# Two head groups taken in turn at the start of an mLSTM, soft-MoE and ReLU² kernel

## The chip, the cores and the metric

One core of a Trainium2 chip runs the whole program. The metric is the device time of one execution in microseconds; less is better.

## The reference

Three layers follow one another on float32 data: an mLSTM over 4 batches of 8 heads (768 steps, head size 40), a soft mixture of experts (8 experts, 4 slots each) and an MLP with a squared ReLU.

```python
for t in range(S):                         # mLSTM, for each batch and head
    m_new = np.maximum(f[t] + m, i[t])
    C = exp(f[t] + m - m_new) * C + exp(i[t] - m_new) * outer(v[t], k[t])
    n = exp(f[t] + m - m_new) * n + exp(i[t] - m_new) * k[t]
    m = m_new
    y[t] = sigmoid(o[t]) * (C @ q[t]) / max(abs(n @ q[t]), 1)
x = y as (3072, 320)
logits = x @ phi                           # soft mixture of experts
slot_in = softmax(logits, over tokens).T @ x
slot_out = relu(slot_in @ w1[e]) @ w2[e]   # e of 8
x = softmax(logits, over slots) @ slot_out
out = relu(x @ w_in)**2 @ w_out            # MLP
```

## The kernel before

The recurrence is computed in chunks of 128 steps, six to a head. The 32 heads form 11 groups of three (the last has two). A **unit** is one chunk of one group; there are 66, and `units` lists them in the order of work: before, group by group, six chunks each. The program writes out the order of every engine's queue by hand; each engine works in that order.

Before any unit, the gates of all heads at once (96 rows: the 32 heads three times) go through phases, for two chunks at a time: `prep(0, 2)`, `prep(2, 4)`, `prep(4, 6)`. The phases have one-letter names: `f` and `m` are scans and `i`, `p`, `a`, `b`, `r`, `l` further steps on VectorE (DVE; some with `G` on GpSimd, POOL), `h`, `A`, `B`, `u`, `v` are passes on ScalarE (ACT), and `q` is a transpose on TensorE (PE) into `qt3`. `D` is a step of the decay (`prep_dec`). The string `START` lists the phases, the steps of the first units and the dummy matmuls (`~n` for n of 128x256, `~~n` for 4n of 40 rows) in order; `|` parts what runs inside the loop, one part at the end of each unit. `M`, `E`, `K`, `T`, `P` with a number are the steps `e_mb`, `e_exp`, `e_sel`, `e_st`, `e_pm` of a unit of group 0.

For unit i the loop emits, in this order: loads for later groups; `e_u(i)`, k times wv (L493); `e_st(i+2)`, keys times queries (L468); `e_mb(i+3)`, the decay products (L437); `e_uc(i)` (L509, L512, VectorE), which takes `u` into the state, and the mask of that state on GpSimd (L528); fillers from later stages; `e_pm(i+2)`, the product of scores and weights (L480, VectorE); `e_exp(i+3)`, three exponentials (L451, ScalarE); `e_av` for two chunks at each second unit (L553); `e_inter(i)` (L538); `e_sel(i+3)`, the causal select (L458, GpSimd); numerators (`e_num`, L571 ScalarE, L572 and L579 VectorE); `e_wv` (L424, GpSimd); the next part of `START`; fillers. `fin` normalises a finished group: `numr` (L613) on GpSimd, then x on VectorE (L622).

PSUM has eight banks here: two each for `mb`, `st` and `o`, one for `m`, one (`ltb`) for the logits, half of which the dummies use. `u` lies in the spare last quarter of the `st` bank of unit i+2.

Group g keeps keys in block-diagonal form (`kbd`), queries, v and k in `par[g % 2]`. A group's keys, queries, v and k are 360, 384, 369 and 360 KB, the two gate files 288 KB each. All DMAs are issued by SyncE (SP) in program order. x arrives per batch, its sigmoid is made on ScalarE (`sigm`, L651), w_in arrives in ten pieces in `stage` and is narrowed (`win_all`, L140 to L152) as the last of the fillers, w1 in sixteen halves (`ring` for experts' first column half, `ring2` for the second) from unit 17 on. Behind the units come the routing of the last batch, the expert layers (w2 reloads `ring` after the first up-projection, L123) and the last MLP (L1387), which is half of the time.

Of the kernel before, what the change touches and what calls it, by code (L numbers as in the profile page):

```python
# [22 lines left out]
GL = 3  # L23
# [9 lines left out]
WO = (4, 5, 9)  # L33
START = "~42 1f 1i 1m 1h 1p 1b 1B 1aG 1r 2f 1u 1A 1v 1q 1l M0 2iG E0 M1 K0 W T0 T1 2m E1 K1 3f 2p 2b 2a ~24 2h 3i 3m 2B Z0 2r 2A 2v 2u P0 3p 3bG D0 3h Z1 ~3 2q ~~5 2l M2 E2 D0 P1 3a 3A 3B K2 D0 D0 3r 3u D0 | 3l 3v 3q | D1 D1 | D1 D1 D1 |"
REBIAS = 2.0**-112
# [7 lines left out]
def kernel(  # L43
# [80 lines left out]

    w1q = [(i, p) for i in range(8) for p in range(2)]

# [64 lines left out]
    ltb = ps.tile([128, 512], F32, name="ps_lt")  # L191
    dum = ltb[:, 256:512]
# [6 lines left out]
    def warm64(n):  # L199
        t = bank("m")  # L200
        for w in (128, 41):
            for _ in range(n):
                for o, r in ((dum, 0), (t, 64)):
                    a = ident[r : r + 40]
                    nc.tensor.matmul(o[:, 0:w], lhsT=a, rhs=a[:, 0:w], start=True, stop=True)

# [14 lines left out]

    def load_kv(g):
        h0, nh = groups[g]
        o = 4 * S
        for dst, src, w in ((vin, v_s, DV), (kin, k_s, D)):
            t = par[g % 2][:, o : o + NC * nh * w]
            o += NC * 3 * w
            dst[g] = t.rearrange("p (c n d) -> p c n d", c=NC, d=w)
            nc.sync.dma_start(out=t, in_=src[S * w * h0 : S * w * (h0 + nh)].rearrange("(p f) -> p f", p=128))

# [49 lines left out]
    nc.sync.dma_start(out=ig.rearrange("p c s -> p (c s)"), in_=i_gate)  # L280
    nc.vector.memset(kbd[0][:, :, 0 : S // 2], 0.0)
    nc.vector.memset(kbd[0][:, :, S // 2 : S], 0.0)
    for cs in (slice(0, S // 2), slice(S // 2, S)):
        load_kb(0, cs)
        load_q(0, cs)
    load_kv(0)
    nc.sync.dma_start(out=phs, in_=phi)
# [29 lines left out]
    nc.vector.tensor_copy(sel96, selF[0:96])  # L317
    nc.vector.tensor_reduce(out=gmask, in_=gj, axis=AX.X, op=ALU.add)
    nc.vector.tensor_reduce(out=gs3, in_=gj.rearrange("p g j -> p j g"), axis=AX.X, op=ALU.add)
    nc.vector.tensor_copy(hsel, gs3.unsqueeze(2).to_broadcast([32, 3, D]))  # L320
    nc.vector.tensor_copy(sel4, selF.unsqueeze(1).to_broadcast([128, 4, 32]))

# [3 lines left out]
    fc = gt(96, [NC, L])  # L326
    dec = gt(32, [NC, 1])
    q3, mm, r1 = ig, fg, dl

    def prep(c0, c1):  # L330
# [11 lines left out]
        def qt():  # L342
            t = bank("o")
            for c in range(c0, c1):
                nc.tensor.transpose(t[:, 96 * (c - c0) : 96 * (c - c0) + 96], q3[:, c, :], ident[0:96, 0:96])
            nc.scalar.copy(qt3[:, cs, :], t[:, 0 : 96 * w].rearrange("p (c s) -> p c s", s=96))
# [69 lines left out]
    ws, pms, pos, cus, cbds = {}, {}, {}, {}, {}  # L416
    units = [(g, c) for g in range(NG) for c in range(NC)]
    NU = len(units)
# [14 lines left out]
    def e_mb(g, c):  # L433
        h0, nh = groups[g]
        mb = bank("mb")
        for j in range(nh):
            nc.tensor.matmul(  # L437
                mb[:, 128 * j : 128 * j + 128],
                lhsT=sel96[:, h0 + j : h0 + j + 1].to_broadcast([96, 128]),
                rhs=M3[:, 128 * c : 128 * c + 128],  # L440
                start=True,
                stop=True,
            )
        mbs[g, c] = mb
# [17 lines left out]
    def e_st(g, c):  # L462
        nh = groups[g][1]
        nd = nh * D
        st = stk.pop(units[max(units.index((g, c)) - 2, 0)], None) or bank("st")
        ts_ = slice(128 * c, 128 * c + 128)
        for j in range(nh):
            nc.tensor.matmul(  # L468
                st[:, 128 * j : 128 * j + 128],
                lhsT=kbd[g % 2][0:nd, j, ts_],  # L470
                rhs=qin[g][0:nd, ts_],
                start=True,
                stop=True,
            )
        sts[g, c] = st
# [12 lines left out]
    def e_u(g, c):  # L488
        nh = groups[g][1]
        nd, nv = nh * D, nh * DV  # L490
        stk[g, c] = bank("st")
        u = stk[g, c][:, 384:512]
        nc.tensor.matmul(  # L493
            u[0:nd, 0:nv],
            lhsT=kin[g][:, c].rearrange("p n d -> p (n d)"),
            rhs=wvs.pop((g, c)).rearrange("p n d -> p (n d)"),
            start=True,
            stop=True,
        )
        us[g, c] = u  # L500

    def e_uc(g, c):
        nh = groups[g][1]
        nd, nv = nh * D, nh * DV
        uv = us.pop((g, c))[0:nd, 0:nv].rearrange("p (n d) -> p n d", d=DV)
        hv = hm[0:nd, 0:nh].unsqueeze(2).to_broadcast([nd, nh, DV])
        cb = wk.tile([120, nh, DV], F32, tag="cbd", name="cbd", bufs=2)
        if c == 0:
            nc.vector.tensor_tensor(out=cb[0:nd], in0=uv, in1=hv, op=ALU.mult)  # L509
        else:  # L510
            cu = wk.tile([120, nh, DV], F32, tag="cu", name="cu", bufs=1)
# [12 lines left out]

# [36 lines left out]
    def e_num(g, c):  # L561
# [282 lines left out]

    def start_exp(c):
        e_mb(0, c)
        e_exp(0, c)
        e_sel(0, c)
# [30 lines left out]
    for i, (g, c) in enumerate(units):  # L879
        if c == NC - 2 and 0 < g + 2 < NG:  # L880
            load_kb(g + 2)
        if i == 0:
            load_kb(1)
        if c == 0 and g + 1 < NG:
            load_q(g + 1)
        if c == 1 and g + 1 < NG:
            load_kv(g + 1)
        if i == 0:
# [23 lines left out]
        if i + 3 < NU:  # L912
            e_mb(*units[i + 3])
# [37 lines left out]
        if i in (0, 2):
            e_wv(0, i + 2, i + 4)
        elif i > 2 and i + 3 < NU and units[i + 3][1] % 3 == 0:
            e_wv(units[i + 3][0], units[i + 3][1], units[i + 3][1] + 3)
        if start:
            run(start.pop(0))
        filler(END, i >= LI)
# [531 lines left out]
```

## Time and profile before

| | |
|---|---|
| three runs | 394.40, 395.84, 396.88 us; median 395.84 |
| profiled execution | 396.85 us, of which the trace's span is 395.1 |
| PE busy | 383.2 us (97%) |
| DVE busy | 264.7 us (67%) |
| ACT busy | 251.9 us (64%) |
| POOL busy | 103.6 us (26%) |
| HBM read | 52.10 MB |

The span runs from the first to the last instruction; 1.75 us of the profiled execution lie outside it. The busy shares are means over stages of quite different kinds, so the rows below are taken by stretch. The chain that ended last runs over PE for 81% of the span.

### The profile page before, as it was taken

The numbers are of one execution on the slowest core, as the hardware profiler recorded it, in microseconds if no ns is written. First come the engines' busy times: TensorE is split into PE (matmuls) and PEld (weight loads), VectorE is DVE, ScalarE is ACT, GpSimd is POOL, SyncE is SP. The second block draws the span as 40 slices with busy tenths as digits, with TensorE's granted clock in tenths as the row PEclk, the third lists the DMA queues.
The fourth block names the chain that finished last, engine by engine and source line by source line (L and its number), as shares of the span: only waits on it lengthen the run. The fifth ranks groups of instructions, "written<-read, shape, count | busy, mean of one in ns | idle before, by whom it ended". The sixth has DMA issues, their size and how long they took to land.

```text
span 395.1 us, 9288 instructions
## 1 busy us (share of the span) xinstructions
PE 383.2 (97%) x3497; PEld 339.0 (86%) x3497; DVE 264.7 (67%) x612; ACT 251.9 (64%) x575; POOL 103.6 (26%) x208
## 2 busy tenths in 40 slices
PE   7998999999999999999998999999999999999996
PEld 5897898889889885534688999999999999999996
DVE  8846787878988786447699856555655655655551
ACT  3676765768677752335598776676666667667662
POOL 6554767747676646200000000000000000000000
PEclk9989999999999999999999999999999999999999
DMA  6577568789889879989100020010001001001001
GB/s 198 171 236 255 190 205 294 268 301 331 275 290 327 238 258 339 327 315 423 73 1 2 0 68 1 2 66 2 1 13 55 2 0 68 0 2 66 2 0 66
DMA packets 18665, 56.62 MB, mean 143 GB/s; under 512 B 2357, under 2 KB 6181, under 8 KB 18237
## 3 DMA queue, kind: packets, MB, share of 16 engines
q1 hardware_dynamic: 18621, 56.04, 41.4%
q8 instruction: 27, 0.44, 0.5%
q14 instruction: 17, 0.14, 0.1%
HBM read 52.10 MB, written 3.93 MB: 142 GB/s over the span
## 4 chain that ended last, share of the span: by engine, by line
PE 81%; DMA 5%; DVE 4%; ACT 3%; POOL 2%; issue 2%; SPq 0%; DVEq 0%; ACTq 0%; POOLq 0%
PE ps_mb L1387 17%; PE ps_st L1387 15%; PE ps_st L468 9%; PE ps_lt L1387 8%; PE ps_o L553 5%; PE ps_o L538 4%; PE ps_o L1311 4%; DMA ring<-in_w_dram 3%; PE ps_st L493 3%; PE ps_mb L437 2%; PE ps_m L668 2%; PE ps_m L1311 2%; PE ps_lt L674 2%; DMA stage<-in_w_in_dram 2%; PE ps_st L1099 1%
## 5 line engine op out<-in xcount | busy, mean ns | idle before, releaser
L1334 DVE CAST hi<-ring 128x512 fp32r<-128x512 f32 x91 | 38.8, 427 | 60.7 <-ACT ring L1333 50.7
L1335 DVE TENSOR_TENSOR lo<-ring,hi 128x512 fp32r<-128x512 f32 x96 | 66.5, 693 | 10.0
L451 ACT ACTIVATE w<-ps_mb,qt 128x128 f32<-128x128 f32 x192 | 56.9, 372 | 23.7 <-PE ps_mb L437 19.4
L1316 ACT ACTIVATE ring<-ps_o 128x512 f32<-128x512 f32 x65 | 38.9, 598 | 36.6 <-PE ps_o L1311 36.5
L1333 ACT ACTIVATE ring<-ring 128x512 f32<-128x512 f32 x91 | 57.5, 632 | 2.9
L468 PE MATMUL ps_st<-par 120*128 120x128 f32 (+1 forms) x384 | 54.6, 278 | 0.0
L1387 PE MATMUL ps_mb<-wohlh,hi 128*128 128x320 f32 x160 | 49.6, 311 | 0.0
L1387 PE MATMUL ps_mb<-wohlh,lo 128*128 128x320 f32 x160 | 49.5, 310 | 0.0
L1387 PE MATMUL ps_mb<-wohll,hi 128*128 128x320 f32 x160 | 49.3, 309 | 0.0
L468 PEld LDWEIGHTS ps_st<-par 120*128 120x128 f32 (+1 forms) x384 | 48.6, 193 | 0.5 <-issue 0.5
L458 POOL TENSOR_SCALAR_AFFINE_SELECT w<-w 128x384 f32<-128x384 f32 (+1 forms) x66 | 36.9, 561 | 37.6 <-ACT w L451 29.3
L1387 PE MATMUL ps_st<-wohlh,hi 128*128 128x320 f32 x144 | 44.8, 311 | 0.0
L1387 PE MATMUL ps_st<-wohlh,lo 128*128 128x320 f32 x144 | 44.7, 310 | 0.0
L1387 PE MATMUL ps_st<-wohll,hi 128*128 128x320 f32 x144 | 44.6, 310 | 0.0
L480 DVE TENSOR_TENSOR p<-ps_st,w 128x384 f32<-128x384 f32 (+1 forms) x66 | 35.5, 538 | 5.3 <-POOL w L458 4.3
L1387 PEld LDWEIGHTS ps_mb<-wohll,hi 128*128 128x128 f32 x160 | 30.1, 188 | 1.3
L1316 ACT ACTIVATE ring<-ps_m 128x512 f32<-128x512 f32 x31 | 18.6, 599 | 18.8 <-PE ps_m L1311 18.8
L1387 PEld LDWEIGHTS ps_mb<-wohlh,hi 128*128 128x128 f32 x160 | 30.0, 188 | 0.0
L1387 PEld LDWEIGHTS ps_mb<-wohlh,lo 128*128 128x128 f32 x160 | 30.0, 188 | 0.0
L553 PE MATMUL ps_o<-par,p 128*64 128x41 f32 x768 | 29.4, 233 | 0.0
L553 PEld LDWEIGHTS ps_o<-par,p 128*64 128x64 f32 x768 | 25.5, 139 | 3.6 <-issue 0.4
L538 PE MATMUL ps_o<-cbd,par 120*128 120x123 f32 (+1 forms) x110 | 25.6, 315 | 3.0 <-POOL cbd L528 2.7
(271 smaller groups left out, 796.3 us busy)
## 6 DMA issues: line engine op xcount, KB each, us to landing
ring<-in_w_dram SPq DMA_DIRECT2D x24, 640.0 KB
stage<-in_w_in_dram SPq DMA_DIRECT2D x10, 512.0 KB
par<-in_w_dram SPq DMA_DIRECT2D x6, 640.0 KB
out_dram<-ring SPq DMA_DIRECT2D x24, 160.0 KB
par<-in_v_s_dram SPq DMA_DIRECT2D x10, 369.0 KB
par<-in_k_s_dram SPq DMA_DIRECT2D x10, 360.0 KB
par<-in_k_t_dram SPq DMA_DIRECT2D x29, 120.0 KB
par<-in_q_t_dram SPq DMA_DIRECT2D x9, 384.0 KB
```

The costliest lines, as they stand in the source:

```text
L451: nc.scalar.activation(w[:, j, :], mb[:, 128 * j : 128 * j + 128], AF.Exp, bias=qt3[:, c, h0 + j : h0 + j + 1])
L458: nc.gpsimd.affine_select(out=w, in_=w, pattern=[[0, nh], [1, 128]], compare_op=ALU.is_ge, fill=0.0, base=0, channel_multiplier=-1)
L468: nc.tensor.matmul(st[:, 128 * j : 128 * j + 128], lhsT=kbd[g % 2][0:nd, j, ts_], rhs=qin[g][0:nd, ts_], start=True, stop=True,)
L480: nc.vector.tensor_tensor(out=p, in0=sts.pop((g, c))[:, 0 : nh * 128].rearrange("p (n t) -> p n t", n=nh), in1=ws.pop((g, c)), op=ALU.mult,)
L538: nc.tensor.matmul(pos[g, c // 2][:, o0 : o0 + nv], lhsT=qin[g][0:nd, 128 * c : 128 * c + 128], rhs=cbds[g, c - 1][0:nd], start=True, stop ...
L553: nc.tensor.matmul(po[t0 : t0 + 64, o0 : o0 + DV], lhsT=p[:, j, t0 : t0 + 64], rhs=vin[g][:, c, j, :], start=True, stop=True,)
L1311: nc.tensor.matmul(t, lhsT=gst[n][:, 128 * k : 128 * k + 128], rhs=cst[tg], start=True, stop=True)
L1316: nc.scalar.activation(r, t, AF.Relu)
L1333: nc.scalar.activation(r, r, AF.Square)
L1334: nc.vector.tensor_copy(hi, r)
L1335: eng.tensor_tensor(out=lo, in0=r, in1=hi.bitcast(F32), op=ALU.subtract)
L1387: nc.tensor.matmul(acc[u][:, 0:DM], lhsT=l_[:, 128 * u : 128 * u + 128], rhs=wohl[r_, f // 8][:, f % 8, :], start=(f == 0 and a == 0), sto ...
```

## The change

The order of units becomes g0c0, g0c1, g1c0, g1c1, g0c2, g0c3, g1c2, g1c3, g0c4, g0c5, g1c4, g1c5, and from group 2 on as before. Group 1's arrays are loaded at the start beside group 0's, group 2's in two pieces at units 6 and 10. Three of the four zero fills of `kbd` are made on ScalarE (a copy scaled by 0). `START` does the phases of chunks 0 to 3, all but `2q`, ahead of the loop and spreads the rest over units 0 to 6; its part in each unit now runs ahead of `e_pm`. It has fewer dummies: 24 + 6 + 6 instead of 42 + 24 + 3 and 20 of 40 rows. `u` moves into the last quarter of the `mb` bank of unit i+3, and `e_mb(i+3)` now stands right behind `e_u(i)`, ahead of `e_st(i+2)`. The gates' transposes use `ltb` instead of an `o` bank. The numerators of groups 0 and 1 lie in `ring`, which w1 fills after `ring2` now; two state buffers for each of the two groups lie in `ring` too. `sigm(0)` is added at unit 4 instead of 0, `win_all` at unit 8 instead of 5.

```diff
-START = "~42 1f 1i 1m 1h 1p 1b 1B 1aG 1r 2f 1u 1A 1v 1q 1l M0 2iG E0 M1 K0 W T0 T1 2m E1 K1 3f 2p 2b 2a ~24 2h 3i 3m 2B Z0 2r 2A 2v 2u P0 3p 3bG D0 3h Z1 ~3 2q ~~5 2l M2 E2 D0 P1 3a 3A 3B K2 D0 D0 3r 3u D0 | 3l 3v 3q | D1 D1 | D1 D1 D1 |"
+START = "~24 1f 1i 1m 1h 1p 1b 1aG 1B 1r 1u 1A 1v D0 S 2f 1l T0 T1 1q M0 2i E0 W0 K0 D0 M1 E1 ~6 2m D0 2p 2b 2aG K1 W2 P0 2h D0 2B 2r 2u P1 M2 E2 2A 2v 2l K2 | 3f 3i ~6 | 2q 3m 3h 3p | 3b 3aG 3B D1 3r | 3u 3A 3l D1 3v D1 D1 | 3q D2 | D2 | D2 D2 X |"
...
-    w1q = [(i, p) for i in range(8) for p in range(2)]
+    w1q = [(i, p) for i in (4, 5, 6, 7, 0, 1, 2, 3) for p in range(2)]
...
-    nc.vector.memset(kbd[0][:, :, S // 2 : S], 0.0)
-    for cs in (slice(0, S // 2), slice(S // 2, S)):
-        load_kb(0, cs)
-        load_q(0, cs)
-    load_kv(0)
+    for g, cs in ((1, halves[0]), (0, halves[1]), (1, halves[1])):
+        z = kbd[g][:, :, cs]
+        nc.scalar.activation(z, ident[0 : 3 * D, 0:1].unsqueeze(2).to_broadcast(list(z.shape)), AF.Copy, scale=0.0)
+    for g in range(2):
+        load_kb(g, halves[0])
+        load_q(g, halves[0])
+        load_kv(g)
+    for g in range(2):
+        load_kb(g, halves[1])
+        load_q(g, halves[1])
...
-            t = bank("o")
+            t = ltb
...
-    units = [(g, c) for g in range(NG) for c in range(NC)]
+    units = [(g, c0 + c) for c0 in range(0, NC, 2) for g in range(2) for c in range(2)]
+    units += [(g, c) for g in range(2, NG) for c in range(NC)]
...
-        mb = bank("mb")
+        mb = mbk.pop((g, c), None) or bank("mb")
...
-        st = stk.pop(units[max(units.index((g, c)) - 2, 0)], None) or bank("st")
+        st = bank("st")
...
-        stk[g, c] = bank("st")
-        u = stk[g, c][:, 384:512]
+        n = units.index((g, c)) + 3
+        t = bank("mb")
+        if n < NU:
+            mbk[units[n]] = t
+        u = t[:, 384:512]
...
+            if g < 2:
+                nums[g] = ring[:, NC * nh * DV * g : NC * nh * DV * (g + 1)].rearrange("p (c n d) -> p c n d", c=NC, n=nh)
+            else:
+                nums[g] = tp.tile([128, NC, nh, DV], F32, tag="num", name="num")
...
+        if i in (6, 10):
+            cs = (0, 4) if i == 6 else (4, NC)
+            load_kb(2, slice(L * cs[0], L * cs[1]))
+            load_q(2, slice(L * cs[0], L * cs[1]))
+            load_kv(2, *cs)
...
         if c < NC - 1:
             e_u(g, c)
+        if i + 3 < NU:
+            e_mb(*units[i + 3])
         if i + 2 < NU:
             e_st(*units[i + 2])
...
-        if i == 5:
+        if i == 8:
             add(win_all(), "win")
...
         if MID:
             filler(MID)
+        if start:
+            run(start.pop(0))
         if i + 2 < NU:
             e_pm(*units[i + 2])
```

## Rows read from the trace of the kernel before

**Rows 1.** Stretches: each engine's busy us (x instructions), granted clock, DMA share, GB/s.
```profile
2.13:17.41 15.28, 14.32 (x135) 12.08 (x133) 14.01 (x37) 6.87 (x22) 9.16 (x24) 1.00 0.64 201
17.41:26.98 9.57, 9.21 (x101) 8.41 (x100) 4.82 (x16) 8.16 (x25) 4.38 (x9) 0.82 0.70 232
26.98:44.17 17.19, 15.19 (x204) 13.98 (x201) 11.26 (x29) 11.21 (x34) 11.13 (x22) 1.00 0.67 220
44.17:142.00 97.83, 97.67 (x1277) 86.74 (x1275) 80.51 (x208) 67.75 (x211) 66.98 (x127) 1.00 0.84 276
142.00:172.00 30.00, 28.59 (x280) 16.81 (x281) 18.53 (x72) 10.87 (x32) 10.55 (x21) 1.00 0.86 301
```

**Rows 2.** VectorE in order of time: start us, us, then what.
```profile
2.44 1.02 DVE L282 MEMSET par<- 120x1152 f32 x1 [0.31 <-DVE par L281]
...
25.57 0.29 DVE L572 TENSOR_TENSOR tmp<-ps_o,qt 128x123 f32<-128x123 f32 x1 [0.42 <-ACT num L571]
...
26.43 0.55 DVE L480 TENSOR_TENSOR p<-ps_st,w 128x384 f32<-128x384 f32 x1
```

**Rows 3.** TensorE in order of time: `u` of units 0, 4, 12.
```profile
17.41 0.47 PE L493 MATMUL ps_st<-wv,par 128*120 128x123 f32 x2
...
27.32 0.38 PE L493 MATMUL ps_st<-wv,par 128*120 128x123 f32 x2
...
44.17 0.37 PE L493 MATMUL ps_st<-wv,par 128*120 128x123 f32 x2
```

**Rows 4.** Who waited for whom, 12 to 45 us: in total, times, longest.
```profile
DVE cu L512 <- PE ps_st L468: 4.4, 4, 1.5
...
PE ps_o L538 <- POOL cbd L528: 1.9, 2, 1.4
```

**Rows 5.** The chain that ended last, in order of time: start us, us, what.
```profile
20.09 1.29 PE ps_st L468 x6
...
27.18 6.40 DMA stage<-in_w_in_dram
...
62.01 0.21 PE ps_st L493 x2
62.22 0.67 PE ps_st L468 x6
62.89 0.17 PE ps_mb L437 x3
63.06 0.83 PE ps_o L553 x24
63.89 0.41 PE ps_o L538 x2
...
65.36 0.27 PE ps_o L538 x2
...
172.48 12.83 DMA ring<-in_w_dram
```

**Rows 6.** Two single microseconds, columns as in rows 1.
```profile
20.00:21.00 1.00, 1.00 (x7) 1.00 (x7) 0.00 (x0) 0.95 (x4) 0.57 (x2) 0.50 0.97 260
168.00:169.00 1.00, 1.00 (x12) 0.26 (x8) 0.94 (x3) 0.00 (x0) 0.00 (x0) 1.00 0.21 87
```

**Rows 7.** ScalarE in order of time, 20 to 36 us.
```profile
21.16 0.74 ACT L651 ACTIVATE x<-x 128x640 f32<-128x640 f32 x1
...
33.60 0.66 ACT L140 ACTIVATE wi<-stage 128x512 f32<-128x512 f32 x1 [3.03 <-DMA stage<-in_w_in_dram]
```

**Rows 8.** All engines, 87 to 90 us.
```profile
88.73 0.88 ACT L451 ACTIVATE w<-ps_mb,qt 128x128 f32<-128x128 f32 x3
...
89.23 0.34 DVE L512 SCALAR_TENSOR_TENSOR cu<-cbd,dec,ps_st 120x123 f32<-120x123 f32 x1 [0.29 <-POOL cbd L528]
```

**Rows 9.** GpSimd in order of time, 0 to 46 us.
```profile
11.54 0.59 POOL L424 TENSOR_TENSOR wv<-par,qt 128x246 f32<-128x246 f32 x1
...
39.41 1.14 POOL L613 TENSOR_TENSOR numr<-num,rc 128x240 f32<-128x240 f32 x2
```

More of the change, by code (lines that the diff above doesn't have):

```diff
@@ L191 @@
     ltb = ps.tile([128, 512], F32, name="ps_lt")
-    dum = ltb[:, 256:512]
+    dum = ltb[:, 0:256]
     zb = ident.bitcast(BF16)
@@ L197, in warm @@
             nc.tensor.matmul(dum if t is None else t[:, 0:256], lhsT=zb[:, 0:128], rhs=zb, start=True, stop=True)
[L199 to L205, printed above, removed]
     kin, vin, xb = {}, {}, {}
@@ L220, in load_q, with load_kv @@
         nc.sync.dma_start(out=par[g % 2][0:n, 3 * S : 4 * S][:, cs], in_=q_t[h0 * D : h0 * D + n, cs])
-    def load_kv(g):
+    def load_kv(g, c0=0, c1=NC):
         h0, nh = groups[g]
@@ L228, in load_kv @@
             dst[g] = t.rearrange("p (c n d) -> p c n d", c=NC, d=w)
-            nc.sync.dma_start(out=t, in_=src[S * w * h0 : S * w * (h0 + nh)].rearrange("(p f) -> p f", p=128))
+            fs = slice(c0 * nh * w, c1 * nh * w)
+            nc.sync.dma_start(
+                out=t[:, fs], in_=src[S * w * h0 : S * w * (h0 + nh)].rearrange("(p f) -> p f", p=128)[:, fs]
+            )
     def load_x(b, cs):
@@ L280 @@
     nc.sync.dma_start(out=ig.rearrange("p c s -> p (c s)"), in_=i_gate)
-    nc.vector.memset(kbd[0][:, :, 0 : S // 2], 0.0)
-    nc.vector.memset(kbd[0][:, :, S // 2 : S], 0.0)
-    for cs in (slice(0, S // 2), slice(S // 2, S)):
-        load_kb(0, cs)
-        load_q(0, cs)
-    load_kv(0)
+    halves = slice(0, S // 2), slice(S // 2, S)
+    nc.vector.memset(kbd[0][:, :, halves[0]], 0.0)
+    for g, cs in ((1, halves[0]), (0, halves[1]), (1, halves[1])):
[8 more added lines that the diff above has]
+        load_q(g, halves[1])
     nc.sync.dma_start(out=phs, in_=phi)
@@ L317, with selectors @@
     nc.vector.tensor_copy(sel96, selF[0:96])
[L318 to L321, printed above, removed]
+    def selectors():
+        nc.vector.tensor_reduce(out=gmask, in_=gj, axis=AX.X, op=ALU.add)
+        nc.vector.tensor_reduce(out=gs3, in_=gj.rearrange("p g j -> p j g"), axis=AX.X, op=ALU.add)
+        nc.vector.tensor_copy(hsel, gs3.unsqueeze(2).to_broadcast([32, 3, D]))
     def flat(t):
@@ L327 @@
     dec = gt(32, [NC, 1])
+    cb01 = {(g, p): gt(120, [3, DV]) for g in range(2) for p in range(2)}
     q3, mm, r1 = ig, fg, dl
@@ L506, in e_uc @@
         hv = hm[0:nd, 0:nh].unsqueeze(2).to_broadcast([nd, nh, DV])
-        cb = wk.tile([120, nh, DV], F32, tag="cbd", name="cbd", bufs=2)
+        cb = cb01[g, c % 2] if g < 2 else wk.tile([120, nh, DV], F32, tag="cbd", name="cbd", bufs=2)
         if c == 0:
@@ L521, in e_uc @@
         cbds[g, c] = cb
-    masks, stk = [], {}
+    masks, mbk = [], {}
     def e_mask():
@@ L565, in e_num @@
         if c == 1:
-            nums[g] = tp.tile([128, NC, nh, DV], F32, tag="num", name="num")
+            if g < 2:
+                nums[g] = ring[:, NC * nh * DV * g : NC * nh * DV * (g + 1)].rearrange("p (c n d) -> p c n d", c=NC, n=nh)
+            else:
+                nums[g] = tp.tile([128, NC, nh, DV], F32, tag="num", name="num")
         pv = po[:, 0 : 4 * nv].rearrange("p (k c n d) -> p k c n d", k=2, c=2, n=nh)
@@ L843 @@
     w2p = [par[a][:, HS * n : HS * n + HS] for a in (1, 0) for n in range(3)]
[L845 to L848, printed above, removed]
     begin = {"1": prep(0, 2), "2": prep(2, 4), "3": prep(4, NC)}
-    pds = [prep_dec(0, 4), prep_dec(4, NC)]
-    begin["W"] = lambda: e_wv(0, 0, 2)
+    pds = [prep_dec(c, c + 2) for c in range(0, NC, 2)]
+    begin["W"] = lambda n: e_wv(units[int(n)][0], 0, 2)
+    begin["S"] = selectors
+    begin["X"] = lambda: nc.vector.tensor_copy(sel4, selF.unsqueeze(1).to_broadcast([128, 4, 32]))
     begin["D"] = lambda n: next(pds[int(n)], None)
-    begin["Z"] = lambda h: nc.gpsimd.memset(kbd[1][:, :, S // 2 * int(h) : S // 2 * (int(h) + 1)], 0.0)
     def run(seq):
         for ch in seq.split():
-            if ch[:2] == "~~":
-                warm64(int(ch[2:]))
-            elif ch[0] == "~":
+            if ch[0] == "~":
                 warm(int(ch[1:]))
             elif ch[0] in "MEKTP":
-                {"M": e_mb, "E": e_exp, "K": e_sel, "T": e_st, "P": e_pm}[ch[0]](0, int(ch[1:]))
+                {"M": e_mb, "E": e_exp, "K": e_sel, "T": e_st, "P": e_pm}[ch[0]](*units[int(ch[1:])])
             elif ch[0] in "123":
@@ L879 @@
     for i, (g, c) in enumerate(units):
-        if c == NC - 2 and 0 < g + 2 < NG:
-            load_kb(g + 2)
[L882 to L888, printed above, removed]
+        if i in (6, 10):
[3 more added lines that the diff above has]
+            load_kv(2, *cs)
+        if g and c == NC - 2 and g + 2 < NG:
+            load_kb(g + 2)
+        if g > 1 and g + 1 < NG:
+            if c == 0:
+                load_q(g + 1)
+            if c == 1:
+                load_kv(g + 1)
+        if i == 4:
             add(sigm(0), ("sig", 0))
@@ L908 @@
             add(sigm(b), ("sig", b))
-        if i == 5:
+        if i == 8:
             add(win_all(), "win")
         advance("W")
-        if i + 3 < NU:
-            e_mb(*units[i + 3])
         if c < NC - 1:
@@ L930 @@
             g1, c1 = units[i - 1]
-            while c1 == 1 and g1 > 1 and ("fin", g1 - 2) not in done:
+            while c1 == 1 and g1 > 3 and ("fin", g1 - 2) not in done:
                 for ph in "WAgGD":
@@ L939 @@
                     add(fin(g1), ("fin", g1), [("sig", b) for b in batches(g1)])
-        elif i > 1 and (c > 1 and g < NG - 1 or c == 1 and g <= GL):
+                nm = None
+        elif i > 1 and nm:
             finish(nm)
-            if c == 1:
-                add(fin(g - 1), ("fin", g - 1), [("sig", b) for b in batches(g - 1)])
+            g1, c1 = units[i - 2]
+            if c1 == NC - 1:
+                add(fin(g1), ("fin", g1), [("sig", b) for b in batches(g1)])
         elif g == NG - 1 and c > 1:
@@ L950 @@
                     next(f1)
[L951 to L956, printed above, removed]
+        if i + 3 < NU:
+            g3, c3 = units[i + 3]
+            if g3 < 2 and i % 2:
+                e_wv(g3, c3, min(c3 + 2, NC - 1))
+            elif g3 > 1 and c3 % 3 == 0:
+                e_wv(g3, c3, c3 + 3)
         filler(END, i >= LI)
```

## Prediction

> **What bounds the kernel now.** I read four views, coarse to fine. First the stages [rows 1]. From 44.17 to 142 us TensorE is busy 97.67 of 97.83 us; the reader is to see that nothing else can bound this stage, so that a time won before it arrives at its end whole, unless the change makes a new wait. The start is different: in 2.13 to 17.41 VectorE is busy 14.01 of 15.28 us, in 17.41 to 26.98 only 4.82 of 9.57, and in 26.98 to 44.17 no engine is full (TensorE 15.19 of 17.19). Then VectorE's order of work [rows 2]: it fills `kbd[0]` in two halves, works through the gate phases, and reaches the product for unit 5 (`p` L480) only at 26.43. Then TensorE's order [rows 3]: `u` of unit 0 starts at 17.41 us, that of unit 4 at 27.32, that of unit 12 at 44.17. Last the chain that ended last [rows 5], which in the steady stage shows what a pair of units costs TensorE: a pair's `av` 0.83 us, `inter` 0.41 + 0.27, and twice `u` 0.21, `st` 0.67, `mb` 0.17, in all 3.61 us, and of the start shows the one long wait, 6.40 us for a piece of w_in from 27.18.
>
> So the head has two faults. Unit 0 waits until the gates of all six chunks are nearly done, though it needs only chunk 0; and once units run, VectorE sits idle waiting for TensorE 4.4 us in four waits for `u` [rows 4], while TensorE has nothing ready to do.
>
> **A, units 0 to 3 begin earlier.** VectorE's work up to the end of the product for unit 5 is the same before and after, less one fill. From 2.13 to 26.98 us it is busy 14.01 + 4.82 = 18.83 us and idle 6.02 [rows 1]. The second fill of `kbd[0]` (1.02 us, [rows 2]) goes to ScalarE; the two fills of `kbd[1]` go from GpSimd to ScalarE as well. ScalarE is busy 6.87 + 8.16 = 15.03 of these 24.85 us [rows 1], and a 640-column pass costs it 0.74 us [rows 7], so three fills of 1152 columns cost at most 3 x 0.74 x 1152/640 = 4.0 us, less three 0.74 us passes of `sigm(0)` that move behind unit 4: 16.8 us against the 20 that VectorE needs. ScalarE hides them; if they ran into the first gate phase they would delay it by under 1 us: they can start when ScalarE's table is loaded, at about 2 us, and the first phase that ScalarE has comes some 4 us later. VectorE's remaining 17.8 us, without a gap, would end at 19.9 instead of 26.98: 7.1 us is the ceiling. The gaps go because the order is now chunk 0-1 gates, units 0 to 3 on them, and chunks 2-3 and 4-5 between those units; and because `u` moves out of the bank of `st`: now `uc` starts when the six `st` matmuls behind `u` have ended, which is most of the four waits in [rows 4]; after the change it waits for the three `mb` matmuls, 0.17 instead of 0.67 us. Some gaps stay: the gate files' landing, hand-overs to ScalarE of each phase, `mprev` and decay. I take 2 us of idle left, so 5.0 us won; the other end is 4 us of idle left, 3.0 won. `u` of unit 0 itself can come at about 11 us: its `wv` was ready at 12.13 before [rows 9], and VectorE starts the gates a fill (1.3 us with its gap) earlier; before, it stood in TensorE's order behind dummies and the later chunks' phases. What is late next is TensorE: units 4 on at its own pace.
>
> The loads move too. Group 1's four arrays are queued by SP right behind group 0's first half, some 1.1 MB more before the second halves and x. In 2.13 to 17.41 us DMA ran 201 GB/s at a share of 0.64 [rows 1], so some 310 GB/s with a full queue; the gates (0.58 MB) and both groups' half of keys and queries with all of v and k (1.1 MB each) are 2.8 MB, 9 us from about 2 us on as an estimate, so in by 11 to 12 us, just when the second `wv` (units 2 and 3) can be made. If it landed 2 us late it would hold GpSimd's queue (select of unit 2 behind it) by as much; that is inside the 3.0 end.
>
> **B, units 4 to 11.** Before, 44.17 - 27.32 = 16.85 us [rows 3]. At 3.61 us a pair, less two `u` and one `inter` that these units don't have (0.42 + 0.27), TensorE needs 13.75. The 3.1 us between are mainly the w_in piece: ScalarE stood 3.03 us before L140 [rows 7], the exponentials queue behind it in order, and TensorE ran dry. In the changed order w_in is asked for at unit 8 instead of 5, and SP can issue it soon after group 2's first piece, with fewer loads ahead of it (group 1 has long landed). But units also come faster, and SP now waits for unit 5's matmuls before group 2's q and for unit 9's before its second piece, and w_in stands behind the first of these. Ends 0 and 3.1; I take half, 1.5.
>
> **C, the TensorE clock.** In 20 to 21 us the granted clock was 0.50, 1.2 GHz, after a stretch of 40-row dummies and a short idle gap, and six `st` matmuls took 1.29 us instead of 0.67 [rows 5, 6]. The change cuts the dummies from 42 + 24 + 3 + 20 to 24 + 6 + 6, and TensorE will stand idle between its first 24 dummies and the first loads and gates. A dip like the one before is in the baseline already. Ends: +0.8 (none any more) to -3 (rival 1); I take -0.5.
> By the Trainium skill, "TensorE: Matmul & The Clock Gate", Part 1, the low clock is the idle default and only activity releases it; this speaks against removing dummies, and by it the time is that of rival 1. The trace agrees so far as it shows a fall in the one stretch with thin work.
>
> **D, two `fin` close together.** Group 0 now ends at unit 9 and group 1 at unit 11, so the two sets of `numr` on GpSimd meet (two take 1.14 us, [rows 9]), with masks queued behind them, and `inter` of the next unit waits for the mask. Ends 0 and -1.9 (what the wait for the `cbd` masks cost TensorE in the head before, [rows 4]); I take -0.5.
>
> **E, after unit 12.** Order and loads are as before, with `mb` ahead of `st`. Three small things cost nothing that I can see: the numerators in the ring are read before w1 comes there, as the second ring is now filled first; the half of w1 that the first up-projection reads is now loaded last, but asked for at unit 62, still inside the unit loop, and read only after the last routing step; the select-matrix copy at unit 6 is 0.2 us on VectorE, under TensorE's bound. The end of the attention part gains up to 0.8 (shorter `u` to mask) and can lose up to 1.5: the eight w2 loads that the chain waits 12.83 us for [rows 5] queue behind everything asked for earlier, and DMA was at a share of only 0.21 just before them [rows 6], so a backlog of some 1 to 1.5 us can still be absorbed. I take 0.
>
> Sum: 5.0 + 1.5 - 0.5 - 0.5 = 5.5 us. The profiled execution took 396.85 us, so 391.35; it lies 1.0 above the median of the three runs, 395.84, from which the same gain gives **390.3 us**. About 1% (4 us) is what a measurement of this kernel can tell from no change.
>
> **Rival 1: the head stays slow on TensorE.** Fewer dummies leave it at 1.2 GHz through units 0 to 3. Two pairs then cost 14.4 instead of 7.2 us; starting at about 11 us, unit 4 comes at about 26, and A shrinks to 1.3; with B at 1.5 and D the gain is 2 to 3 us: 393.3. For: thin work was followed by a fall once [rows 6]. Against: the clock was full from 2.13 to 17.41 us with 1 us idle in it [rows 1]. Chance 0.2.
>
> **Rival 2: slower, by the shared bank.** ScalarE's and VectorE's reads of one bank already go one after the other: the first product `tmp` waited 0.42 us for ScalarE's copy [rows 2], though it needs nothing from it but the bank. Now `uc` (VectorE) and the exponentials of three units later (ScalarE) read one bank, so the exponentials wait for `uc`. Where VectorE lags this bites: in one unit the exponentials began at 88.73 and `uc` ran only at 89.23 to 89.57 [rows 8]; they would start 0.84 us later. Each unit has some 2 us of reserve (product two units ahead), so mostly nothing comes of it. It decides at 5.5/54 = 0.1 us a unit over units 12 to 65: with 0.2 the kernel takes 395.84 - 5.5 + 10.8 = 401. Chance 0.1, half of it slower than before by over 1%.
> The Trainium skill, "PSUM — Partial Sum Buffer", "PSUM bank collisions raise a hardware error", says two engines may not touch one bank and quadrant at once, reads included; the wait in the trace agrees.
>
> **Rival 3: given back behind the attention.** Transfers are near their limit from 142 us on: a share of 0.86 up to 172 [rows 1], then the 12.83 us wait [rows 5]. If all that was won before meets a full queue, the time is 394 to 396. Against: the idle slot at 168 us [rows 6], and that every load is tied to units, which move together. Chance 0.1.
>
> **How the numbers follow.** Forecast 0.6 (386.8 to 391.9, all of A and B at one end), rivals 0.2, 0.1, 0.1. The range 386.8 to 395.0 takes in rivals 1 and most of 3. Faster by over 1%: 0.6 and the best of rival 1, 0.64; slower: 0.07; the rest 0.29.
>
> **What would show it.** `u` of unit 0 at 11 to 12 us, of unit 4 at 22 to 23, of unit 12 at 37 to 39; VectorE's idle up to the product of unit 5 down from 6.0 to about 2; `uc` no longer waiting for `st`; no 3 us wait at L140; from there to the end the same intervals as before. Wrong if the granted clock stays 0.5 beyond one dip, if a row of exponentials waits for `uc` with TensorE idle behind it, or if the wait for w2 grows by what was won.

## The result: slower, and the profile after

Four runs of the changed kernel took 399.49 to 402.92 us, median 400.88; the kernel before, run beside it, had a median of 395.65. The ratio is 1.013 [1.009, 1.017]: slower by 5.2 us, where 5.5 us faster was forecast. The profiled execution of after took 399.49 us with a span of 397.8, 2.7 longer than the 395.1 of before; it is the shortest of its four runs, while the 396.85 of before is near the longest of its own, so the two traces show only half of the difference. Both profiled executions had a mean granted clock of 0.995; the three longer runs of after had 0.991, 0.991 and 0.987.

First the start of units, which was the heart of the forecast. TensorE's order of work after, `u` of units 0, 4, 12 and 14:

```profile
11.87 0.44 PE L500 MATMUL ps_mb<-wv,par 128*120 128x123 f32 x2 [0.45 <-ACT w L455]
...
23.96 0.38 PE L500 MATMUL ps_mb<-wv,par 128*120 128x123 f32 x2
...
39.68 0.38 PE L500 MATMUL ps_mb<-wv,par 128*120 128x123 f32 x2
...
43.36 0.38 PE L500 MATMUL ps_mb<-wv,par 128*120 128x123 f32 x2
```

Against [rows 3] unit 0 comes 5.5 us earlier, unit 4 3.4 and unit 12 4.5; unit 14 started at 48.40 before, so it comes 5.0 earlier. But `u` of unit 62, before and then after:

```profile
147.97 0.30 PE L493 MATMUL ps_st<-wv,par 128*80 128x82 f32 x2
```

```profile
147.56 0.30 PE L500 MATMUL ps_mb<-wv,par 128*80 128x82 f32 x2
```

4.6 of the 5.0 us are gone ahead of the end of the attention part, 3.5 of them by unit 24 (units 14 to 24 took 19.64 us before and 23.17 after). TensorE's groups from unit 14 to unit 62 show where. Columns: busy us, mean ns, then idle time before and its releaser. Before (48.40 to 147.97 us):

```profile
L468 PE MATMUL ps_st<-par 120*128 120x128 f32 (+1 forms) x280 | 39.4, 276 | 0.0
...
L538 PE MATMUL ps_o<-cbd,par 120*128 120x123 f32 (+1 forms) x80 | 18.6, 314 | 0.2
...
L668 PE MATMUL ps_m<-ident,x 128*120 128x128 f32 (+1 forms) x54 | 8.9, 274 | 0.0
L674 PE MATMUL ps_lt<-xTw,phs 120*32 120x256 f32 (+1 forms) x51 | 5.5, 390 | 0.0
```

After (43.36 to 147.56 us):

```profile
L472 PE MATMUL ps_st<-par 120*128 120x128 f32 (+1 forms) x280 | 41.6, 284 | 0.0
...
L545 PE MATMUL ps_o<-cbd,par 120*128 120x123 f32 (+1 forms) x82 | 18.4, 306 | 1.9 <-POOL cbd L535 1.9
...
L678 PE MATMUL ps_m<-ident,x 128*120 128x128 f32 (+1 forms) x60 | 9.9, 273 | 0.0
L684 PE MATMUL ps_lt<-xTw,phs 120*32 120x256 f32 (+1 forms) x54 | 5.7, 391 | 0.0
```

The reader is to see three things. First, `st` costs 284 ns instead of 276, 2.2 us over 280 matmuls; that is the order `mb` ahead of `st`. Second, `inter` waits 1.9 us for masks, which stand on GpSimd behind the `numr` of groups 0 and 1. GpSimd, then TensorE, after:

```profile
44.41 1.14 POOL L623 TENSOR_TENSOR numr<-ring,rc 128x240 f32<-128x240 f32 x2
...
46.11 0.48 PE L545 MATMUL ps_o<-cbd,par 120*128 120x123 f32 x2 [1.49 <-POOL cbd L535]
```

Before also waited 1.9 us for masks, ahead of unit 14 [rows 4], but mostly for another reason. GpSimd, then TensorE, before:

```profile
35.11 0.52 POOL L458 TENSOR_SCALAR_AFFINE_SELECT w<-w 128x384 f32<-128x384 f32 x1 [3.94 <-ACT w L451]
...
36.81 0.48 PE L538 MATMUL ps_o<-cbd,par 120*128 120x123 f32 x2 [1.39 <-POOL cbd L528]
...
41.11 0.48 PE L538 MATMUL ps_o<-cbd,par 120*128 120x123 f32 x2 [0.46 <-POOL cbd L528]
```

The 1.39 us belong to a mask behind a select that waited for exponentials, and these stood behind the w_in piece of [rows 7]; only 0.46 us were behind a `numr` [rows 9]. Third, six transposes with their logits, 1.2 us, which before did between 43.73 and 48.40 us, just ahead of unit 14, come behind unit 14 in after.

2.2 + 1.9 + 1.2 is 5.3 for a loss of 4.6, because the 2.2 are not a net loss: `inter` is 0.2 us shorter with two matmuls more, and the kernel before with that order alone loses 0.8 us from unit 14 to unit 62 (below). So of the 5.0 us "won" at unit 14, 1.2 were work not yet done, and 1.9 were lost again in waits that before did not have behind this point.

Then the end. The windows behind the attention part, columns as in [rows 1]. Before:

```profile
143.00:158.00 15.00, 14.18 (x141) 9.63 (x140) 10.86 (x44) 5.51 (x18) 7.96 (x18) 1.00 0.90 311
...
172.00:176.00 4.00, 4.00 (x40) 1.35 (x36) 2.63 (x5) 1.48 (x3) 0.00 (x0) 1.00 1.02 415
```

After:

```profile
143.00:158.00 15.00, 14.63 (x147) 10.11 (x147) 11.38 (x45) 6.50 (x20) 7.24 (x19) 1.00 0.50 175
158.00:172.00 14.00, 13.42 (x116) 5.89 (x119) 5.20 (x24) 2.54 (x8) 1.75 (x1) 1.00 0.90 350
172.00:176.00 4.00, 1.12 (x10) 0.26 (x2) 1.72 (x3) 2.18 (x4) 0.00 (x0) 0.96 1.02 418
176.00:179.00 3.00, 3.00 (x16) 1.05 (x19) 1.91 (x3) 1.22 (x3) 0.00 (x0) 0.50 1.01 413
```

Transfers idle half of 143 to 158 us (share 0.50, 0.90 before), then run full, and TensorE, busy all of 172 to 176 before, works 1.12 us of it and then three more at half its clock. SP's issues say why. Before:

```profile
120.22 0.33 SPq L168 DMA_DIRECT2D stage<-in_w_in_dram  x1
...
143.08 1.76 SPq L123 DMA_DIRECT2D stage<-in_w_dram  x2
...
158.98 0.33 SPq L981 DMA_DIRECT2D wo<-in_w_out_dram  x1
```

After:

```profile
129.49 0.35 SPq L168 DMA_DIRECT2D stage<-in_w_in_dram  x1
...
158.47 1.02 SPq L123 DMA_DIRECT2D stage<-in_w_dram  x2
...
160.67 0.37 SPq L993 DMA_DIRECT2D wo<-in_w_out_dram  x1
```

The last piece of w_in is asked for 9 us later, so `stage`, which w2 reuses, comes free 15 us later; two w2 loads of 640 KB, with two more in order behind them, go out just ahead of the first piece of w_out. The chain that ended last waits for that piece, where before, behind the attention, it waited at [rows 5]'s last line:

```profile
160.67 10.90 DMA wo<-in_w_out_dram
...
171.68 0.82 ACT par L140
172.50 0.69 ACT par L144
...
173.21 0.84 DVE par L148
...
174.07 0.83 DVE wo L152
174.90 0.08 DVE rt L1133
...
175.00 0.70 ACT x L1116
...
175.74 1.12 PE ps_mb L1160 x4
```

The narrowing of w_out stands ahead of the routing factor (`rt`) and the first ReLU (L1116) on VectorE and ScalarE, and TensorE's transposes (L1160) wait for the ReLU. The last MLP, half of the time, begins at 195.64 us instead of 193.09: from 0.4 earlier at unit 62 to 2.6 later, so 3.0 us were lost behind the attention.

### The profile page after: what moved, and what is told of

Same layout as the page of the kernel before. It is cut to its first block, busy times and chain, and to the rows that moved or that the text cites. A ratio compares the mean times of both kernels' runs of the same rounds, so it can differ in the third digit from the quotient of the medians.

```text
span 397.8 us, 9181 instructions
## 1 busy us (share of the span) xinstructions
PE 379.0 (95%) x3426; PEld 333.9 (84%) x3426; DVE 265.8 (67%) x614; ACT 254.0 (64%) x579; POOL 101.0 (25%) x207
## 4 chain that ended last, share of the span: by engine, by line
PE 80%; DVE 6%; ACT 4%; DMA 4%; issue 2%; POOL 2%; SPq 0%; DVEq 0%; ACTq 0%; POOLq 0%
PE ps_mb L1399 16%; PE ps_st L1399 15%; PE ps_st L472 9%; PE ps_lt L1399 8%; PE ps_o L560 6%; PE ps_o L545 4%; PE ps_o L1323 4%; PE ps_mb L500 3%; DMA wo<-in_w_out_dram 3%; PE ps_st L1179 2%; PE ps_mb L441 2%; PE ps_m L1323 2%; PE ps_lt L684 2%; PE ps_m L678 2%; ACT w L455 1%
## 5 line engine op out<-in xcount | busy, mean ns | idle before, releaser
L472 PE MATMUL ps_st<-par 120*128 120x128 f32 (+1 forms) x384 | 56.9, 284 | 2.1 <-DMA par<-in_q_t_dram 1.7
L462 POOL TENSOR_SCALAR_AFFINE_SELECT w<-w 128x384 f32<-128x384 f32 (+1 forms) x66 | 38.4, 582 | 41.0 <-ACT w L455 33.6
L1399 PEld LDWEIGHTS ps_st<-wohll,hi 128*128 128x128 f32 x144 | 27.1, 188 | 1.3
```

The lines of the kernel that those rows point to most:

```text
L462: nc.gpsimd.affine_select(out=w, in_=w, pattern=[[0, nh], [1, 128]], compare_op=ALU.is_ge, fill=0.0, base=0, channel_multiplier=-1)
L472: nc.tensor.matmul(st[:, 128 * j : 128 * j + 128], lhsT=kbd[g % 2][0:nd, j, ts_], rhs=qin[g][0:nd, ts_], start=True, stop=True,)
L1399: nc.tensor.matmul(acc[u][:, 0:DM], lhsT=l_[:, 128 * u : 128 * u + 128], rhs=wohl[r_, f // 8][:, f % 8, :], start=(f == 0 and a == 0), sto ...
```

## The experiments

The theory after these readings (T in the first expectations) had three losses: the two `fin` on GpSimd together with exponentials that stand behind `uc` (units 14 to 24), `mb` ahead of `st` (some 1 us), and the late w_in (3 to 4 us). The rival (R) was rival 2 of the prediction, the shared bank alone. In the expectations from "both steps together" on, low-clock stretches in the head took the place of the first loss. Each kernel ran beside the kernel before; the ratio is to that.

**w_in at unit 5 in the changed kernel.**

```diff
-        if i == 8:
+        if i == 5:
             add(win_all(), "win")
```

> The changed kernel with w_in begun at unit 5 again. Theory T: the changed kernel lost in three places, and the last one is that w_in ends one piece later (158.4 us instead of 143), so that four w2 loads stand ahead of the first piece of w_out and a ReLU waits behind its narrowing on ScalarE; then the last pieces move forward by 10 us or more, the 2.9 us wait of TensorE before L1160 and the 0.50 clock behind it go, and the time falls by 3 to 4 us, to about 397.5. Rival R (the exponentials' wait for uc in the shared bank is the whole loss): the time stays at 401.

Measured: 396.92 us (12 runs), 1.0026 [0.9997, 1.0055], 4.0 less than after, as T said. SP's issues:

```profile
118.60 1.34 SPq L168 DMA_DIRECT2D stage<-in_w_in_dram  x1
...
141.38 1.10 SPq L123 DMA_DIRECT2D stage<-in_w_dram  x2
...
157.19 0.33 SPq L993 DMA_DIRECT2D wo<-in_w_out_dram  x1
```

The wait at L1160 is gone, and 172 to 179 us are full at the full clock. The profiled execution had no low-clock stretch until TensorE's work was done, and a span of 393.4, 4.4 less than after: 0.7 by unit 14, the rest behind unit 62.

**The same step alone in the kernel before**, `win_all` at unit 8 instead of 5.

> The kernel before with only w_in asked for at unit 8 instead of 5. Theory (late w_in holds the w2 and w_out loads in SP's queue): last w_in narrowing some 10 us or more later, w2's first loads at 150 us or later instead of 143, a wait of 2 to 3 us at the first ReLU or the transposes behind it, 398.5 to 400. Rival (the tail's loss belongs to the new order of units and loads): 395.7, w2 loads as before; the 3 us wait of ScalarE for w_in in the head could even shrink.

Measured: 401.27 us (6 runs), 1.0131 [1.0092, 1.0170]: this one number makes the old kernel as slow as the changed one. ScalarE, then TensorE:

```profile
174.00 0.81 ACT L140 ACTIVATE par<-wo 128x640 f32<-128x640 f32 x1 [8.97 <-DMA wo<-in_w_out_dram]
```

```profile
178.02 0.66 PE L1148 MATMUL ps_mb<-ident,x 128*128 128x128 f32 x4 [3.37 <-ACT x L1104]
```

The loss is 5.5 us, above the 4 expected, but not all of it is the wait: the granted clock also fell at 43 to 47 us in its profile, five of the six runs had a mean clock under 0.998, and the sixth took 398.55. Both directions say that w_in's start is the largest single cost.

**`u` and the order of `st` and `mb`.** Three kernels: the changed one with `e_mb` behind `e_st`; the same with `u` back in the `st` bank; and before with `e_mb` ahead of `e_st`. The first edit, and in words the others:

```diff
-        if i + 3 < NU:
-            e_mb(*units[i + 3])
         if i + 2 < NU:
             e_st(*units[i + 2])
+        if i + 3 < NU:
+            e_mb(*units[i + 3])
```

> The changed kernel with the decay products again behind the scores (u, st, mb), all else as changed. Theory T: each set of six st matmuls costs 0.72 us behind mb and 0.67 behind u, so st falls to 0.67, about 3 us less over 60 units, of which some is eaten by the later wait of uc: 398 to 399. Rival R: st stays at 0.72 whatever stands ahead, and since uc and the exponentials come later by the st time, the kernel gets no faster: 401 or more.

Measured: 407.43 us (6 runs), 1.0293 [1.0253, 1.0333]: T missed by 8 to 9, and R's "401 or more" holds for the time but not for `st`. `st` fell back to 276 ns as T said, but the clock was at half in three stretches of the profile, one of which is

```profile
155.00:169.00 14.00, 14.00 (x81) 8.58 (x80) 6.99 (x25) 2.32 (x9) 5.99 (x12) 0.51 0.18 51
```

with TensorE busy throughout. All six runs had a mean clock of 0.969 to 0.983. Why the clock falls there in this kernel is not settled, so its median can't price the order. Units 24 to 62 ran at full clock, though: they took 81.70 us, against 81.03 in after, so with `u` in the `mb` bank the old order is no gain.

> The changed kernel with u in the bank of st again and the decay products behind the scores, so exponentials no longer share a bank with uc. Theory T: as with the order alone (st 0.67), and about 1 us more because the exponentials no longer wait in units 14 to 20; w_in still ends late: 397 to 398. Rival R: the whole gain of the head comes through, 395.65 - 5 = 390.5.

Measured: 400.96 us (6 runs), 1.0120 [1.0080, 1.0159]: neither T nor R. Its profile has the clock at half in 14 to 17 and 24 to 31 us, ahead of unit 14. From unit 14 to unit 62 it took 102.11 us against 104.20 of after and 99.57 of before. Its groups there:

```profile
L472 PE MATMUL ps_st<-par 120*128 120x128 f32 (+1 forms) x280 | 39.4, 276 | 0.0
...
L542 PE MATMUL ps_o<-cbd,par 120*128 120x123 f32 (+1 forms) x82 | 19.1, 315 | 1.3 <-POOL cbd L532 1.3
```

What is left against before is 1.3 of wait and the 1.2 of work put off, 2.5, as measured. Units 24 to 62 took 79.92 us, as before (79.93), and against the 81.70 of the kernel above only the bank differs, so in this order the shared bank costs 1.8 us there. So the step saves 2.1 us from unit 14 to unit 62, and the median hides it.

> The kernel before with only the decay products moved ahead of the scores (u, mb, st); no bank is shared anew. Theory T: st costs 0.72 instead of 0.67 in each unit, and TensorE bounds the stage: 2.5 to 3 us more, 398.4. Rival R: no shared bank, so no loss: 395.7.

Measured: 398.07 us (12 runs), 1.0057 [1.0034, 1.0080], near T's 398.4. Its `st` in 70 to 140 us:

```profile
L468 PE MATMUL ps_st<-par 120*128 120x128 f32 x192 | 28.4, 284 | 0.0
```

The same 284 ns, without any shared bank of `u` and `mb`; units 24 to 62 took 80.71 us instead of 79.93, and units 14 to 24 no more than before (19.66, 19.64). `inter` fell from 314 to 303 ns and gives part of it back. Only these 0.8 of the 2.3 us are shown to be the order's; 4 of its 12 runs had a mean clock under 0.998.

**Both steps together**: `u` in the `st` bank with the order of before, w_in at unit 5.

> The changed kernel with u back in the st bank, the PE order u, st, mb of before, and w_in asked for at unit 5. Theory (three separate losses: st placed behind mb on TensorE costs some 1.5 us up to unit 62, the late w_in some 4 us at the tail, and low-clock stretches in the head that come in some runs): no wait at the last narrowing, six st matmuls at 276 ns each as before, span near 391.5 at full clock, median 395 to 395.7. Rival (the u,mb,st order costs nothing, as the first trial of u in st alone gave no gain in the median): 397, as with w_in at unit 5 alone.

Measured: 395.63 us (12 runs), 1.0003 [0.9977, 1.0029], as the theory said. But 11 of the 12 runs had a mean clock under 0.998; the one at 0.998 took 392.78. In the profile TensorE stood before the decay's matmul (L408), and then the clock fell. The order of work, then the window:

```profile
22.42 0.59 PE L408 MATMUL ps_m<-ring 32*120 32x22 f32 x2 [2.46 <-DVE ring L400]
```

```profile
21.00:29.00 8.00, 6.58 (x51) 6.39 (x52) 3.15 (x11) 3.40 (x13) 2.90 (x7) 0.57 0.49 191
```

**More dummies where TensorE waits**, w_in at 5. Fragments of `START`:

```diff
-~24 1f
+~34 1f
-2v 2l K2 | 3f 3i ~6 |
+2v 2l K2 ~4 | 3f 3i ~9 |
-| 3u 3A 3l D1 3v
+| ~10 3u 3A 3l D1 3v
```

> The changed kernel with w_in at unit 5 and 27 more dummies put where TensorE waits in the head (10 before the gates, 4 before u of unit 0, 3 after unit 0, 10 before the decay of chunks 2 and 3). Clock theory (the runs of the changed kernel differ by whether the granted clock falls in the head, mean clock 0.987 to 1.000): mean clock 0.998 or more in nearly all runs and median 395.2, 1.7 below w_in at unit 5 alone (396.9). Rival (the dips come from elsewhere, or the dummies stand in the way): 397 or above, clock as spread as before.

Measured: 394.79 us (12 runs), 0.9983 [0.9966, 1.0000], 2.1 less than without them, as the clock theory said. The runs' clocks, here and in kernels below, worked out from each run's record:

```
kernel                           runs  median clock  runs under 0.998  median us
after, w_in at 5                   12         0.995                10     396.92
  with 27 more dummies             12         1.000                 1     394.79
after, w_in at 5, u in st          12         0.987                11     395.63
before, 24 + 6 dummies             12         0.984                12     396.43
27 dummies, w_in at 8               6         0.996                 6     400.04
27 dummies, w_in at 5, one numr    12         1.000                 0     394.90
  and u in st                      12         0.998                 5     393.26
  and w_in at 4                     6         1.000                 0     392.78
```

The wait at L408 fell to

```profile
22.49 0.38 PE L408 MATMUL ps_m<-ring 32*120 32x22 f32 x2 [0.62 <-DVE ring L400]
```

because dummies fill what was idle, at no cost to unit 4 (23.95 us).

**The dummies alone, w_in still at 8.**

> The changed kernel with the 27 more dummies only; w_in stays at unit 8. If the clock and the late w_in are separate losses: mean clock 0.998 or more in most runs up to the tail, 398.8 (400.9 less the 2.1 that the dummies gave with w_in at 5). If the low clock came from the late loads: no gain, 400.9.

Measured: 400.04 us (6 runs), 1.0097 [1.0065, 1.0129], between the two: the gain is 0.8, not 2.1, and the intervals of this kernel and of after overlap. The head is at full clock in the profile, but every run is under 0.998, and in the profile the clock falls where the late loads make TensorE idle:

```profile
172.00:176.00 4.00, 1.37 (x12) 0.79 (x16) 1.73 (x4) 2.18 (x5) 0.00 (x0) 0.95 1.02 419
176.00:179.00 3.00, 3.00 (x20) 0.81 (x16) 2.62 (x5) 0.52 (x2) 0.00 (x0) 0.50 1.03 415
```

So the two losses aren't separate: part of the low clock belongs to the late w_in, and with the dummies in place w_in at 5 is worth 5.3 us (400.04 to 394.79).

**Fewer dummies in the kernel before**: `~42`, `~24`, `~3` and `~~5` of `START` become `~24`, `~6`, none and none.

> The kernel before with 24 + 6 dummies of 256 columns in place of 42 + 24 + 3, and without the 20 x 2 of 40 rows. Clock theory: the granted clock falls in the head in most runs (mean clock under 0.998), 397 to 398.5. Rival (the dummies cost TensorE time ahead of unit 0 and nothing is lost without them): 395.7 or up to 1 us less, clock 0.999 as before.

Measured: 396.43 us (12 runs), 1.0013 [0.9989, 1.0037]: the clock fell in all 12 runs, as the clock theory said, but the time hardly moved, so its 397 to 398.5 missed; the rival had the time within a microsecond and the clock wrong. The windows of its head:

```profile
2.13:17.25 15.12, 10.25 (x56) 8.09 (x54) 13.90 (x37) 7.09 (x23) 9.02 (x24) 0.71 0.64 203
17.25:26.80 9.55, 9.55 (x101) 8.90 (x100) 4.85 (x16) 7.96 (x24) 4.37 (x9) 0.75 0.70 231
```

14 us at half clock, and unit 0 still starts at 17.25 us (17.41 before): VectorE, 13.90 of 15.12 us busy, sets the pace there. The low clock that is free in the old head costs 2.1 us (396.92 to 394.79) to 2.9 us (395.63 to the one run of 392.78) in the new one, where TensorE has units to do.

**One `numr` at a time on GpSimd up to unit 19**, with the dummies, w_in at 5 and `u` in the `st` bank.

```diff
+        GN = 1 if i < 20 else 2
...
-            k = advance(ch, {"P": PL, "A": 2, "D": 2, "G": 2}.get(ch, 1) + (late and ch in LT))
+            k = advance(ch, {"P": PL, "A": 2, "D": 2, "G": GN}.get(ch, 1) + (late and ch in LT))
```

> The changed kernel with u in the st bank and the old PE order, w_in at unit 5, the same 27 more dummies, and at most one numr at a time on GpSimd up to unit 19. If the losses are separate: 393.5 (clock 1.7, order 1.5, and up to 1.3 of the waits of inter for the mask behind two numr, off 396.9 and added to nothing else), inter waits under 0.5 us for the masks of units 14 to 20. If the median's loss has another cause: 396 to 397.

Measured: 393.26 us (12 runs), 0.9952 [0.9930, 0.9974]: faster than both kernels, as the theory said. But `inter`'s wait for masks is 1.3 us, not under 0.5, and no less than with `u` in the `st` bank alone; the gain over the dummies is `u` in the `st` bank and the order together, as the next kernel shows. Five of the 12 runs are still under 0.998.

> The changed kernel with w_in at unit 5, the 27 more dummies and at most one numr at a time up to unit 19; u stays in the mb bank and mb ahead of st. It parts the two edits that took 394.79 to 393.26. If the numr pairs alone make inter wait (and u's bank does not matter): inter's wait 1.9 down to 1.3 us or less, 393.5 to 394.0, with the rest of the step, some 1 us, left to the order of st and mb. If the wait goes through the exponentials that stand behind the uc of the same bank: wait and time as with the dummies alone, 394.8.

Measured: 394.90 us (12 runs), 0.9973 [0.9957, 0.9990]: with `u` in the `mb` bank the limit on `numr` gives nothing, as the second theory said. Who TensorE waited for, 38 to 70 us:

```profile
PE ps_o L545 <- POOL cbd L535: 1.6, 2, 1.2
```

**w_in at unit 4** in the version that took 393.26.

> The version that took 393.26, with w_in asked for at unit 4 instead of 5. If the tail is still ruled by when w_in is through: w2's first loads earlier by some 3 us and up to 1 us faster, 392.3 to 393.3. If w_in at 5 has just enough reserve: 393.3, or slower by up to 3 us where ScalarE waits for the first piece in the head with the exponentials behind it.

Measured: 392.78 us (6 runs), 0.9914 [0.9888, 0.9940], the fastest of all, 392.64 to 392.85. The same view:

```profile
PE ps_o L542 <- POOL cbd L532: 0.7, 2, 0.4
```

The wait for masks halves: a narrowing of w_in (L140) that stood ahead of these exponentials at 40.37 us now runs at 38.21, and the select ahead of the mask begins at 41.25 instead of 41.88. That is read from the traces and was not tried apart. w2 went into `stage` from 116 us on in the version before too. Some 0.2 of the 0.5 us is the clock: the seven runs of that version at 0.998 or more have a median of 393.05. This version keeps the change's order of units and gains 3 us on the kernel before.

## Why the prediction was wrong, step by step

**A, right, at its lower end.** Forecast 3.0 to 5.0. The product of unit 5 ends the head on VectorE:

```profile
23.02 0.55 DVE L484 TENSOR_TENSOR p<-ps_st,w 128x384 f32<-128x384 f32 x1
```

26.43 became 23.02 [rows 2], and unit 4 came 3.4 us earlier, at 23.96 and not 22 to 23. The three fills on ScalarE took 3.25 us where at most 4.0 was allowed.

**B, the number near, half of the reason wrong.** Units 4 to 12 took 15.72 us instead of 16.85, a gain of 1.1 for 1.5; the wait at L140 is 1.51 instead of 3.03 [rows 7]. But w_in at unit 8 has no part in it. With w_in at unit 5 in the changed kernel, L140 runs at 28.99 us without a wait, and these units take 14.96 us; in the old kernel with w_in at 8, L140 still waits 2.47 and they take 17.16. So unit 8 won nothing: in after `mb` (L441) still waited 0.60 us for exponentials behind that piece. The other half of the reason, fewer loads ahead of w_in, was not tried apart. TensorE was busy all of the 14.96 us: its need was not 13.75, and 1.9 was the most that could be won.

**D, mis-sized, and the sum behind it wrong.** The two `fin` cost 1.9, the bound, not 0.5. The bound was the right number by luck: only 0.46 of the 1.9 us in [rows 4] were behind a `numr`, and the other 1.39 came from the w_in piece, as the 0.60 of B did in after. One `numr` at a time took the wait from 1.9 to 1.6 us and won no time, so the `numr` are only a part of what GpSimd has ahead of the mask. The error in the sum is that it took the lead at unit 12 for a lead at the end. Of 5.0 us at unit 14, 1.2 were transposes that before had done by then, and 1.9 went into the new waits. "A time won before it arrives at its end whole" holds only for the same work and, as the prediction said, without a new wait.

**E, the step that failed.** It said that order and loads behind unit 12 are as before and that `mb` ahead of `st` costs nothing. Both are wrong. The order costs 8 ns of each `st` matmul, 2.2 us from unit 14 on, and 0.8 us net by the kernel before with that one edit. And `win_all` at unit 8 was weighed only for what it frees in the head (B), never for what waits for it: `stage` is w2's buffer, SP issues in order, w_out stands behind w2, and the ReLU behind w_out's narrowing. That costs 4.0 us, undone in the changed kernel, and 5.5, done in the old one, the low clock included; 3.0 of it are lost behind unit 62 in the trace of after. E had 0 for all of this. The prediction had seen the full queue (rival 3) and dismissed it since "every load is tied to units, which move together". This one was tied to another unit, and rival 3 priced only what was won being lost, not more.

**C, mis-sized, with a mechanism that was known.** Forecast -0.5. With w_in at 5, filling the gaps with dummies gave 2.1 us (396.92 to 394.79), and runs under 0.998 fell from 10 to 1 of 12; with w_in at 8 they gave 0.8. So rival 1 was a part of the truth, though not in the profiled execution of after, whose head ran at full clock; where the clock fell in its other three runs no trace shows. By the Trainium skill, "TensorE: Matmul & The Clock Gate", Part 1, TensorE's low clock is its idle state and activity releases it; the table of clocks agrees. Read as advice to keep TensorE busy at all times it would count the fewer dummies as a loss in the old head too; the trace there shows the fall but no loss, as VectorE bounds it.

**Rival 2, its time by luck, its mechanism without its price.** It named 401 us, and 400.88 were measured; but it needed 0.2 us in each unit from 12 on, with TensorE waiting behind the exponentials. Units 24 to 62 lost 1.1 us in all (81.03 against 79.93), 0.8 of it by the order alone. In 68 to 145 us of after ScalarE waited for `uc`, as feared:

```profile
ACT w L455 <- DVE cu L519: 12.3, 15, 1.9
ACT w L455 <- DVE cbd L516: 3.0, 4, 1.3
```

19 waits, 15.3 us, and not one wait of TensorE in that stretch, so the reserve of two units took them. The Trainium skill, "PSUM — Partial Sum Buffer", "PSUM bank collisions raise a hardware error", says that ScalarE and VectorE must not be in one bank and quadrant at once; the trace agrees so far as these 19 times the exponentials began only behind `uc`. Between units 14 and 24, where the masks are late, putting `u` back shortened the stretch by 1.0 us (23.17 to 22.19); how much of that is bank and how much order was not parted. With the old order the shared bank did have a price, 1.8 us over units 24 to 62 (81.70 against 79.92).

Together, for the medians: 4.0 for w_in, 2.1 for the clock, 1.5 for `u` with the order of `st` and `mb` (394.79 to 393.26, with the limit on `numr`, which alone gave nothing). 400.88 - 7.6 = 393.3; the sum closes because the steps were taken one on top of the other, and with the dummies first the shares would be 0.8 for the clock and 5.3 for w_in. So without these losses the change is worth 2.5 us to before (395.81 to 393.26, side by side), not 5.5.

## What to carry to other kernels

When an edit shifts the start of a transfer, follow its buffer to the next user and every load behind that in the issuing queue, up to the last one that somebody waits for: the cost can lie 100 us later. Compare two kernels at a point only with the same work done up to it; work put off comes back. Two waits of one size at one line need not have one cause: follow each to what it stands behind. Here TensorE's low clock cost nothing where VectorE set the pace, and began to cost when the change removed that other bound.

## What the runs showed that was not expected

The same fp32 matmul of 120 x 128 took 276 ns behind `u` and 284 ns behind three bf16 `mb` matmuls, in every kernel of either order, while `inter` took 314 to 319 and 303 to 306; why was not tried. Clock falls vary between executions of one kernel: the same program ran with mean clocks of 0.987 to 1.000 and 394.87 to 399.56 us. With the dummies and w_in at 5 it was 394.55 to 396.06, with `u` in the `st` bank besides 392.71 to 395.16, and with w_in at 4 it shrank to 392.64 to 392.85.
